# A fused MLP kernel: other load order, packed transpose banks and late tail transposes in its first 10 microseconds

## The chip, the cores and the metric

The kernel runs on one core of one Trainium2 chip. The metric is the device time of one execution in microseconds (us), lower is better. Times before and after are medians of several executions. The profile shows one execution; its "span" runs from the first to the last instruction on the core and is about 1.7 to 2.2 us shorter than the device time. Engines: PE (matmul), PEld (weight load), DVE (VectorE), ACT (ScalarE), POOL (GpSimd), SP (SyncE, which here issues loads). SBUF and PSUM are the memories named in the code: in these kernels operands lie in SBUF tiles, and PE's results in PSUM tiles, from where other engines copy them.

## The reference

```python
B, S, D, F = 1, 2048, 576, 4608          # all bf16
def reference(x, w1, b1, w2, b2):
    h = jnp.einsum("bsd,df->bsf", x, w1) + b1
    r = jnp.where(h > 0, h, 0)
    h = r * r
    return jnp.einsum("bsf,fd->bsd", h, w2) + b2
```

## The kernel before

The 2048 rows are worked in four blocks of 512. Each block's x must stand transposed in SBUF (tile `xT`, 576 = four chunks of 128 columns and a tail of 64). For blocks 1 to 3 the DMA transposes. Block 0 is loaded plainly and transposed on PE, by intent so that the first matmuls can start early (in the first trace plain x loads landed 2.9 to 3.4 us after issue, DMA transposes 4.0 us, medians). The first group of w1 columns (four blocks of 128, tile `w1n`) is multiplied chunk by chunk while chunks arrive, half of the rows at a time; its 64-row tail is done last by four "tail matmuls", which use 64 rows of the array (64*128 in the timeline below), two at a time (in the first trace both of a pair started at 9.85 us, and both of the next within 0.01 us at 10.07 and 10.08). Then come the other 32 column blocks ("w1 rows", tile `w1_h`), done wholly in such 64-row pairs. For those pairs each 64-column piece of x must stand in both halves of the partitions: DVE duplicates them (`dup_windows`).

The parts that the argument touches (cut, `...` marks cuts):

```python
WARM = [512] * 6 + [128]                       # warm-up matmuls on constants
...
load_x(nc.sync, 0);   load_x(nc.scalar, 1)
load_w1n(nc.sync, 0); load_x(nc.scalar, 2)
load_w1n(nc.sync, 1); load_x(nc.sync, 3)
for k in range(2, NK): load_w1n(nc.sync, k)
...
def dup_windows(sb):
    xT = xT_blk[sb]
    keep(nc.vector.tensor_copy(out=xT[0:H, SPC:SPC + 4, :], in_=xT[H:P, E3:E3 + 4, :]))
    keep(nc.vector.tensor_copy(out=xT[H:P, SPC:SPC + 4, :], in_=xT[0:H, O:O + 4, :]))
...
                # first group; x_transpose(j, k): row tile j, column chunk k; k == NK is the tail
                for j in range(2):
                    for k in range(NK): x_transpose(j, k)
                for j in range(2): x_transpose(j, NK)
                x_copies(0)                    # 3 copies on DVE, 2 on ScalarE
                part(0, 0)                     # part(half of the rows, chunk): 4 matmuls
                for k in range(NK + 1): x_transpose(2, k)
                part(0, 1); part(0, 2)
                for k in range(NK + 1): x_transpose(3, k)
                x_copies(1)
                dup_windows(0)
                part(0, 3); part(1, 0)
                make_b1T()                     # bias transposed on PE
                for k in range(1, NK): part(1, k)
                ...                            # pair(i): the tail matmuls, then evacuation
```

(The lines with several calls are joined here to save room.)

Of the kernel before, what the change touches and what calls it, by code (L numbers as in the profile page):

```python
# [11 lines left out]
BF16 = mybir.dt.bfloat16  # L12
FP32 = mybir.dt.float32
# [4 lines left out]
def kernel(  # L18
# [9 lines left out]
    nc = tc.nc  # L28
    keep = tc.keep_in_program_order
    P = 128  # L30
    H = 64
    x2 = x.flatten_outer_dims()
    out2 = out.flatten_outer_dims()
    S, D = x2.shape
    F = w1.shape[1]
    NFT = F // P
    NC = D // H
    NK = NC // 2
    G = 4
    GW = G * P  # L40
# [4 lines left out]
    RT = SB // P  # L45
    DT = P
    DM = D - DT

    const = ctx.enter_context(tc.tile_pool(name="const", bufs=1))
    wpool = ctx.enter_context(tc.tile_pool(name="wpool", bufs=1))  # L50
# [5 lines left out]
    ps_h = ctx.enter_context(tc.tile_pool(name="ps_h", bufs=4, space=PSUM))  # L56
    ps_o = ctx.enter_context(tc.tile_pool(name="ps_o", bufs=4, space=PSUM))

    wps = ps_o.tile([P, 512], FP32, name="wps", tag="po")
    ones = nc.const_aps.tensor(1.0, [P, 512], BF16)  # L60
    WARM = [512] * 6 + [128]
    for i, n in enumerate(WARM):
        keep(nc.tensor.matmul(wps[:, 0:n], lhsT=ones[:, 0:P], rhs=ones[:, 0:n], start=True, stop=True))  # L63

    xs = const.tile([P, RT, D], BF16, name="x_sb")
    w1n = wpool.tile([P, NK, GW], BF16, name="w1n")
    w1n8 = wpool.tile([P, G // 2, P], BF16, name="w1n8")
    w1_h = wpool.tile([P, NC, FH], BF16, name="w1_h")
    w1_v = w1.rearrange("(c p) f -> p c f", p=H)

    def load_x(eng, rt):
        keep(eng.dma_start(out=xs[:, rt, :], in_=x2[rt * P:(rt + 1) * P, :]))

    def load_w1n(eng, k):
        keep(eng.dma_start(out=w1n[:, k, :], in_=w1[k * P:(k + 1) * P, 0:GW]))

    def load_w1n8(eng, h):
        src = w1[NK * P:D, 0:GW].rearrange("p (i h f) -> p i h f", h=2, f=P)
        keep(eng.dma_start(out=w1n8[h * H:(h + 1) * H, :, :], in_=src[:, :, h, :]))

    def load_w1(eng, h, j0, j1):
        keep(eng.dma_start(out=w1_h[h * H:(h + 1) * H, :, j0 * P:j1 * P],
                      in_=w1_v[:, :, GW + h * FH + j0 * P:GW + h * FH + j1 * P]))

    load_x(nc.sync, 0)
    load_x(nc.scalar, 1)
    load_w1n(nc.sync, 0)
    load_x(nc.scalar, 2)
    load_w1n(nc.sync, 1)
    load_x(nc.sync, 3)  # L90
    for k in range(2, NK):
        load_w1n(nc.sync, k)

    ident = const.tile([P, P], BF16, name="ident")
    make_identity(nc, ident[:])
    b1_rows = const.tile([P, P], BF16, name="b1_rows")
    nc.gpsimd.memset(b1_rows[:], 0.0)
    nc.gpsimd.dma_start(out=b1_rows[0:NFT, :], in_=b1.rearrange("(ft p) -> ft p", p=P))
    b2_col = const.tile([P, 1], BF16, name="b2_col")
    nc.gpsimd.dma_start(out=b2_col[:], in_=b2[DM:D].rearrange("(d o) -> d o", o=1))  # L100
    b2T = const.tile([P, 1], FP32, name="b2T")
    nc.gpsimd.tensor_copy(out=b2T[:], in_=b2_col[:])
    warm = const.tile([P, 1], FP32, name="warm")
    keep(nc.scalar.activation(out=warm[:], in_=nc.const_aps.tensor(0.0, [P, 1], FP32), func=ACT.Relu))

    E3, O, SPC, E = 0, 1, 5, 6
    LO_W = [O, O + 1, O + 2, O + 3, E, E + 1, E + 2, E3, SPC]
# [9 lines left out]
# [4 lines that stand above are left out]
# [7 lines left out]

    w2_sb = wpool.tile([P, NFT, D], BF16, name="w2_sb")
    w2_view = w2.rearrange("(ft p) d -> p ft d", p=P)  # L130
    W2CH = 9

    def load_w2(c):
        keep(nc.sync.dma_start(out=w2_sb[:, c * W2CH:(c + 1) * W2CH, :], in_=w2_view[:, c * W2CH:(c + 1) * W2CH, :]))
# [3 lines left out]
    alloc_xT(0)  # L138
    xT0 = xT_blk[0]
    HS = SB // 2  # L140
    tb_po = [ps_o.tile([P, 2, HS], BF16, name="tb", tag="po") for _ in range(2)]
    tb_ph = [ps_h.tile([P, 2, HS], BF16, name="tb", tag="ph") for _ in range(4)]
    half_banks = [tb_ph, None]

    def x_transpose(j, k):
        h, q = divmod(j, 2)
        qc = slice(q * P, (q + 1) * P)
        bank, slot, c0 = (half_banks[h][k], 0, k * P) if k < NK else (half_banks[h][2], 1, D - P)
        keep(nc.tensor.transpose(bank[:, slot, qc], xs[:, j, c0:c0 + P], ident[:]))  # L149

    def x_copies(h):
        hc = slice(h * HS, (h + 1) * HS)
        for k in range(NK):
            src = half_banks[h][k][:, 0, :]
            if k % 2 == 0:
                keep(nc.vector.tensor_copy(out=xT0[:, O + k, hc], in_=src))  # L156
            else:
                keep(nc.scalar.copy(out=xT0[:, O + k, hc], in_=src))
        keep(nc.vector.tensor_copy(out=xT0[:, E3, hc], in_=half_banks[h][2][:, 1, :]))


    b1T = const.tile([P, NFT], FP32, name="b1T")

    def make_b1T():
        b1T_ps = ps_o.tile([P, P], BF16, name="b1T_ps", tag="po")
        keep(nc.tensor.transpose(b1T_ps[:], b1_rows[:], ident[:]))  # L166
        keep(nc.vector.tensor_copy(out=b1T[:], in_=b1T_ps[:, 0:NFT]))

    hTs = {}

# [24 lines left out]
    def a_full(sb, order):  # L195
        xT = xT_blk[sb]
        banks = []
        for g in range(G):
            pool, tag = (ps_o, "po") if g < 2 else (ps_h, "ph")
            banks.append(pool.tile([P, SB], FP32, name="pn", tag=tag))  # L200

        def pair(i, start, stop):
            keep(nc.tensor.matmul(banks[2 * i][:], lhsT=w1n8[0:H, i, :], rhs=xT[0:H, SPC, :],  # L203
                             start=start, stop=stop, skip_group_check=order == "k_outer"))
            keep(nc.tensor.matmul(banks[2 * i + 1][:], lhsT=w1n8[H:P, i, :], rhs=xT[H:P, E3, :],  # L205
                             start=start, stop=stop, skip_group_check=order == "k_outer"))

        def full(g, k, start, stop):
            keep(nc.tensor.matmul(banks[g][:], lhsT=w1n[:, k, g * P:(g + 1) * P], rhs=xT[:, O + k, :],  # L209
                             start=start, stop=stop))  # L210

        if order == "rows_first":
            for i in (1, 0):
                pair(i, True, False)
            for g in (2, 3, 0, 1):
                for k in range(NK):
                    full(g, k, False, k == NK - 1)
                evac_h(sb, banks[g], g)
        else:
            if order == "k_outer":  # L220
                tb_new = [ps_h.tile([P, 2, HS], BF16, name="tb", tag="ph") for _ in range(2)]
                half_banks[1] = tb_new + tb_po

                def part(h, k):
                    hc = slice(h * HS, (h + 1) * HS)
                    for g in range(G):
                        keep(nc.tensor.matmul(banks[g][:, hc], lhsT=w1n[:, k, g * P:(g + 1) * P],  # L227
                                              rhs=xT[:, O + k, hc], start=(h == 0 and k == 0), stop=False,
                                              skip_group_check=True))

                for j in range(2):
                    for k in range(NK):
                        x_transpose(j, k)
                for j in range(2):
                    x_transpose(j, NK)
                x_copies(0)
                part(0, 0)
                for k in range(NK + 1):
                    x_transpose(2, k)
                part(0, 1)  # L240
                part(0, 2)
                for k in range(NK + 1):
                    x_transpose(3, k)
                x_copies(1)
                dup_windows(0)
                part(0, 3)
                part(1, 0)
                make_b1T()
                for k in range(1, NK):
                    part(1, k)  # L250
            else:
                for g in (2, 3, 0, 1):
                    for k in range(NK):
                        full(g, k, k == 0, False)
            for i in (1, 0):
                pair(i, False, True)
                evac_h(sb, banks[2 * i], 2 * i)
                evac_h(sb, banks[2 * i + 1], 2 * i + 1)
# [35 lines left out]
    for (j0, j1) in [(0, 1), (1, 2), (2, 4), (4, 6), (6, 8), (8, 10), (10, 12)]:  # L294
        load_w1(nc.sync, 0, j0, j1)
        load_w1(nc.sync, 1, j0, j1)
        if j0 == 0:
            load_w1n8(nc.sync, 0)
            load_w1n8(nc.sync, 1)
    load_xT(1)  # L300
    for (j0, j1) in [(12, 14), (14, 16)]:
        load_w1(nc.sync, 0, j0, j1)
        load_w1(nc.sync, 1, j0, j1)
    keep(nc.sync.dma_start(out=b2_bc[:], in_=b2.partition_broadcast(P)))
    for c in (0, 2, 1, 3):
        load_w2(c)
    load_xT(2)

# [51 lines left out]
```

## Time and profile before

| | |
|---|---|
| time, first three runs | 291.02 us median (290.59 to 291.36) |
| span of the profiled run | 289.6 us |
| PE busy | 285.5 us, 99% of the span |
| tail matmuls of the first group start | 9.85 us |

The page's first part for the kernel before (busy time, share of the span, instructions), and its chain that ended last:

```profile
PE 285.5 (99%) x2027; PEld 139.9 (48%) x2032; DVE 78.6 (27%) x176; ACT 96.7 (33%) x154; POOL 2.3 (1%) x10
...
PE 98%; DMA 1%; issue 0%; DVE 0%
```

PE is the bound, almost without gaps. Only the start, before the dense stream of pairs, leaves room. This is the timeline of the kernel before from 3.3 to 11.2 us. Columns: start in us, duration in us, engine, source line, operation, output<-input, shapes, count of merged instructions, and in brackets how long the engine sat idle and what released it. PEld, load issues and the stream of w1 rows are left out.

```profile
3.77 1.25 PE L149 MATMUL tb<-ident,x_sb 128*128 128x128 bf16 x10 [0.17 <-DMA x_sb<-in_x_dram]
4.53 0.29 DVE L156 COPY xTw<-tb 128x256 bf16<-128x256 bf16 x1 [4.53 <-PE tb L149]
...
4.87 1.01 PE L227 MATMUL pn<-xTw,w1n 128*128 128x256 bf16 x4
...
7.24 0.44 PE L149 MATMUL tb<-ident,x_sb 128*128 128x128 bf16 x5
...
7.92 0.28 DVE L159 COPY xTw<-tb 128x256 bf16<-128x256 bf16 x1
...
8.31 0.69 DVE L119 COPY xTw<-xTw 64x2048 bf16<-64x2048 bf16 x1
...
8.44 1.47 PE L227 MATMUL pn<-xTw,w1n 128*128 128x256 bf16 x12
9.03 0.69 DVE L120 COPY xTw<-xTw 64x2048 bf16<-64x2048 bf16 x1
...
9.85 0.39 PE L203 MATMUL pn<-xTw,w1n 64*128 64x512 bf16 x1
```

Three things are to be read. Four 128x256 matmuls took 1.01 us at 4.87 us, but twelve took only 1.47 us at 8.44 us: in between, at 6.5 us by the trace's clock record, PE's clock stepped from half to full (from start to start, 128x256 matmuls took 213, then 109 ns, transposes 107, then 56 ns). The last x transposes (7.24 us) are followed by copies and then by two duplications on DVE. DVE's last duplication ended at 9.72 us, and the tail matmul at 9.85 us shows no idle bracket: DVE was just in time.

### The profile page before, as it was taken

What the parts mean: (1) busy time and instruction counts of PE and PEld (TensorE: products, weight loads), DVE (VectorE), ACT (ScalarE), POOL (GpSimd) and SP (SyncE); (2) the same over time, 40 slices, a digit from 0 to 9 for tenths busy, and PEclk for the clock granted to TensorE, in tenths of its full rate; (3) what the DMA queues carried; (4) which work ended last, traced back from release to release, by engine and by line L of the source; (5) the groups of instructions that cost most, each with busy time, mean ns of one, the idle gap of its engine ahead of it and who ended that gap; (6) DMA issues with size and microseconds to landing.
All of it is one profiled execution on the core that took longest, in us unless ns stands there. A gap on an engine that the chain in (4) does not pass through costs nothing.

```text
span 289.6 us, 4693 instructions
## 1 busy us (share of the span) xinstructions
PE 285.5 (99%) x2027; PEld 139.9 (48%) x2032; DVE 78.6 (27%) x176; ACT 96.7 (33%) x154; POOL 2.3 (1%) x10
## 2 busy tenths in 40 slices
PE   8999999999999999999999999999999999999996
PEld 5544444444444555555544444444444455555555
DVE  1644554444500200000015444444440001100001
ACT  2566666666500000000027666666670000000000
POOL 3000000000000000000000000000000000000000
PEclk9999999999999999999999999999999999999999
DMA  7999999400001200000000000000000110000000
GB/s 198 221 245 188 308 389 212 92 0 2 0 14 25 52 16 18 16 16 18 16 16 2 1 2 0 2 0 2 0 2 0 36 38 16 16 16 19 33 16 18
DMA packets 31605, 16.52 MB, mean 57 GB/s; under 512 B 15700, under 2 KB 31584, under 8 KB 31584
## 3 DMA queue, kind: packets, MB, share of 16 engines
q1 hardware_dynamic: 31232, 15.91, 22.3%
q10 hardware_dynamic: 288, 0.30, 0.4%
q8 instruction: 16, 0.26, 0.4%
q14 instruction: 5, 0.04, 0.0%
q0 software_dynamic: 64, 0.01, 0.0%
HBM read 11.36 MB, written 2.36 MB: 47 GB/s over the span
## 4 chain that ended last, share of the span: by engine, by line
PE 98%; DMA 1%; issue 0%; DVE 0%
PE ph L188 42%; PE po L289 38%; PE pt L270 11%; PE pn L209 4%; PE pn L227 1%; DMA x_sb<-in_x_dram 1%; PE tb L149 1%; PE ph L190 1%; PE pn L203 1%; DVE o_sb L291 0%; PE b1T_ps L166 0%; PE pn L205 0%
## 5 line engine op out<-in xcount | busy, mean ns | idle before, releaser
L190 PE MATMUL ph<-xTw,w_h 64*128 64x512 bf16 x576 | 124.6, 376 | 0.0
L188 PE MATMUL ph<-xTw,w_h 64*128 64x512 bf16 x576 | 124.6, 376 | 0.0
L289 PE MATMUL po<-w_sb,hT 128*128 128x448 bf16 (+2 forms) x612 | 109.4, 341 | 0.0
L176 ACT ACTIVATE r<-ph,b1T 128x512 bf16<-128x512 f32 x128 | 81.1, 685 | 41.6 <-PE ph L190 41.6
L188 PEld LDWEIGHTS <-w_h 64*128 64x128 bf16 x576 | 54.1, 94 | 68.3
L289 PEld LDWEIGHTS <-hT 128*128 128x128 bf16 x612 | 58.5, 98 | 51.0
L177 DVE TENSOR_TENSOR hT<-r 128x512 bf16<-128x512 bf16 x144 | 61.2, 426 | 75.9 <-ACT r L176 75.5
L190 PEld LDWEIGHTS <-w_h 64*128 64x128 bf16 x576 | 54.1, 94 | 0.0
L291 DVE TENSOR_TENSOR o_sb<-po,b_bc 128x448 bf16<-128x448 f32 (+2 forms) x17 | 10.2, 597 | 125.8 <-PE po L289 125.8
L270 PE MATMUL pt<-hT,w_sb 128*128 128x512 bf16 x142 | 31.3, 379 | 0.1
L176 ACT ACTIVATE r<-pn,b1T 128x512 bf16<-128x512 f32 x16 | 10.3, 688 | 61.0 <-PE pn L205 59.6
L270 PEld LDWEIGHTS <-w_sb 128*128 128x128 bf16 x144 | 14.1, 98 | 17.0
L273 ACT ACTIVATE oT<-pt,b2T 128x512 bf16<-128x512 f32 x4 | 2.8, 688 | 28.3 <-PE pt L270 28.3
L209 PE MATMUL pn<-xTw,w1n 128*128 128x512 bf16 x45 | 10.4, 379 | 0.4 <-issue 0.3
L209 PEld LDWEIGHTS <-w1n 128*128 128x128 bf16 x48 | 4.5, 98 | 6.0 <-issue 0.8
L227 PE MATMUL pn<-xTw,w1n 128*128 128x256 bf16 x32 | 4.6, 295 | 0.0
L63 PE MATMUL wps<-const-bfloat16-1.0 128*128 128x512 bf16 (+1 forms) x7 | 2.8, 582 | 0.8 <-PEq L344 0.8
L227 PEld LDWEIGHTS <-w1n 128*128 128x128 bf16 x32 | 3.3, 107 | 0.5
L156 DVE COPY xTw<-tb 128x256 bf16<-128x256 bf16 x4 | 1.1, 292 | 6.7 <-PE tb L149 6.7
L119 DVE COPY xTw<-xTw 64x2048 bf16<-64x2048 bf16 x4 | 2.8, 690 | 0.2
L120 DVE COPY xTw<-xTw 64x2048 bf16<-64x2048 bf16 x4 | 2.7, 687 | 0.1
L149 PE MATMUL tb<-ident,x_sb 128*128 128x128 bf16 x20 | 2.4, 288 | 0.2 <-DMA x_sb<-in_x_dram 0.2
(23 smaller groups left out, 15.2 us busy)
## 6 DMA issues: line engine op xcount, KB each, us to landing
w_sb<-in_w_dram SPq DMA_DIRECT2D x4, 1296.0 KB, 12.7
w_h<-in_w_dram SPq DMA_DIRECT2D x14, 288.0 KB, 6.2
out_dram<-o_sb SPq DMA_DIRECT2D x15, 112.0 KB, 1.7
w_h<-in_w_dram SPq DMA_DIRECT2D x4, 144.0 KB, 3.5
w1n<-in_w_dram SPq DMA_DIRECT2D x4, 128.0 KB, 3.9
out_dram<-ot SPq DMA_DIRECT2D x4, 128.0 KB, 2.0
x_sb<-in_x_dram ACTq DMA_DIRECT2D x2, 144.0 KB, 2.9
x_sb<-in_x_dram SPq DMA_DIRECT2D x2, 144.0 KB, 3.4
```

The costliest lines, as they stand in the source:

```text
L63: keep(nc.tensor.matmul(wps[:, 0:n], lhsT=ones[:, 0:P], rhs=ones[:, 0:n], start=True, stop=True))
L149: keep(nc.tensor.transpose(bank[:, slot, qc], xs[:, j, c0:c0 + P], ident[:]))
L176: keep(nc.scalar.activation(out=r[:], in_=bank[:], func=ACT.Relu, bias=b1T[:, ft:ft + 1], scale=1.0))
L177: keep(nc.vector.tensor_tensor(out=hTs[sb][:, ft, :], in0=r[:], in1=r[:], op=ALU.mult))
L188: keep(nc.tensor.matmul(bx[:], lhsT=w1_h[0:H, LO_C[i], jc], rhs=xT[0:H, LO_W[i], :], start=(i == 0), stop=(i == NC - 1)))
L190: keep(nc.tensor.matmul(by[:], lhsT=w1_h[H:P, UP_C[i], jc], rhs=xT[H:P, UP_W[i], :], start=(i == 0), stop=(i == NC - 1)))
L203: keep(nc.tensor.matmul(banks[2 * i][:], lhsT=w1n8[0:H, i, :], rhs=xT[0:H, SPC, :], start=start, stop=stop, skip_group_check=order == "k_o ...
L209: keep(nc.tensor.matmul(banks[g][:], lhsT=w1n[:, k, g * P:(g + 1) * P], rhs=xT[:, O + k, :], start=start, stop=stop))
L227: keep(nc.tensor.matmul(banks[g][:, hc], lhsT=w1n[:, k, g * P:(g + 1) * P], rhs=xT[:, O + k, hc], start=(h == 0 and k == 0), stop=False, s ...
L270: keep(nc.tensor.matmul(pt[:], lhsT=w2_sb[:, ft, DM:D], rhs=hT[:, ft, :], start=(i == 0), stop=(i == NFT - 1)))
L289: keep(nc.tensor.matmul(po[:, 0:d1 - d0], lhsT=hT[:, ft, jj * P:(jj + 1) * P], rhs=w2_sb[:, ft, d0:d1], start=(i == 0), stop=(i == NFT - 1)))
L291: keep(nc.vector.tensor_tensor(out=o_sb[:, d0:d1], in0=po[:, 0:d1 - d0], in1=b2_bc[:, d0:d1], op=ALU.add))
```

## The change

It reorders the start. x tiles and w1 chunks load in turn on two queues; the tail weights load early; two column chunks share one PSUM bank; the 64 tail columns of two x row tiles go through one transpose (after GpSimd has packed them side by side); and those tail transposes, with the bias, come late in the first group. By intent it saves PE work: 16 x transposes and three for tails and bias, instead of 20 and one. The core of the diff (cut, `...` marks cuts):

```diff
-    WARM = [512] * 6 + [128]
+    WARM = [512] * 6 + [256]
...
-    load_w1n(nc.sync, 0)
-    load_x(nc.scalar, 2)
-    load_w1n(nc.sync, 1)
-    load_x(nc.sync, 3)
-    for k in range(2, NK):
-        load_w1n(nc.sync, k)
+    for k in range(2):
+        load_w1n(nc.sync, k, k + 1)
+        load_x(nc.scalar, 2 + k)
+    load_w1n(nc.sync, 2, 3)
+    load_w1n(nc.scalar, 3, 4)
...
+    for h in range(2):
+        load_w1n8(nc.sync, h)
+    xs8 = const.tile([P, RT, H], BF16, name="xs8")
+    for h in range(2):
+        keep(nc.gpsimd.tensor_copy(out=xs8[:, 2 * h:2 * h + 2, :], in_=xs[:, 2 * h:2 * h + 2, NK * P:D]))
...
-    W2CH = 9
+    W2CH = 18
...
+    def x_transpose(j):
         h, q = divmod(j, 2)
+        hc = slice(h * HS, (h + 1) * HS)
+        for bank in range(2):
+            for k in range(2 * bank, 2 * bank + 2):
+                keep(nc.tensor.transpose(tb[h][bank][:, k % 2, q * P:(q + 1) * P], xs[:, j, k * P:(k + 1) * P], ident[:]))
+            for k in range(2 * bank, 2 * bank + 2) if q == 1 else ():
+                copy = nc.scalar.copy if h == 1 and bank == 1 else nc.vector.tensor_copy
+                keep(copy(out=xT0[:, O + k, hc], in_=tb[h][bank][:, k % 2, :]))
...
+    def dup_windows_first():
+        keep(nc.vector.tensor_copy(out=xT0[0:H, E:E + 3, :], in_=xT0[H:P, O:O + 3, :]))
+        keep(nc.vector.tensor_copy(out=xT0[H:P, SPC:SPC + 4, :], in_=xT0[0:H, O:O + 4, :]))
+        keep(nc.vector.tensor_copy(out=xT0[0:H, E3, :], in_=xT0[H:P, O + 3, :]))
+
+    def tails_and_b1T():
+        tl = ps_h.tile([P, 3, P], BF16, name="tl", tag="ph")
+        for h in range(2):
+            keep(nc.tensor.transpose(tl[:, h, :], xs8[:, 2 * h:2 * h + 2, :], ident[:]))
+        keep(nc.tensor.transpose(tl[:, 2, :], b1_rows[:], ident[:]))
+        x8 = xT0.rearrange("p c (h q t) -> p c h q t", h=2, q=2)
+        for q in range(2):
+            keep(nc.vector.tensor_copy(out=x8[H:P, E3, :, q, :], in_=tl[q * H:(q + 1) * H, 0:2, :]))
+        for q in range(2):
+            keep(nc.vector.tensor_copy(out=x8[0:H, SPC, :, q, :], in_=tl[q * H:(q + 1) * H, 0:2, :]))
+        keep(nc.vector.tensor_copy(out=b1T[:], in_=tl[:, 2, 0:NFT]))
...
                 for j in range(2):
+                    x_transpose(j)
+                for k in range(2):
+                    part(0, k)
+                    x_transpose(2 + k)
+                dup_windows_first()
+                for k in range(2, NK):
+                    part(0, k)
                 part(1, 0)
-                make_b1T()
+                tails_and_b1T()
                 for k in range(1, NK):
                     part(1, k)
```

The tail matmuls read all four pieces that the four new "tail copies" write, and those copies stand behind the three duplications in DVE's order.

More of the change, by code (lines that the diff above doesn't have):

```diff
@@ L57 @@
     ps_o = ctx.enter_context(tc.tile_pool(name="ps_o", bufs=4, space=PSUM))
-    wps = ps_o.tile([P, 512], FP32, name="wps", tag="po")
+    wps = ps_h.tile([P, 512], FP32, name="wps", tag="ph")
     ones = nc.const_aps.tensor(1.0, [P, 512], BF16)
-    WARM = [512] * 6 + [128]
+    WARM = [512] * 6 + [256]
     for i, n in enumerate(WARM):
@@ L66 @@
     w1n = wpool.tile([P, NK, GW], BF16, name="w1n")
-    w1n8 = wpool.tile([P, G // 2, P], BF16, name="w1n8")
+    w1n8 = wpool.tile([P, GW], BF16, name="w1n8")
     w1_h = wpool.tile([P, NC, FH], BF16, name="w1_h")
@@ L72, in load_x, with load_w1n @@
         keep(eng.dma_start(out=xs[:, rt, :], in_=x2[rt * P:(rt + 1) * P, :]))
-    def load_w1n(eng, k):
-        keep(eng.dma_start(out=w1n[:, k, :], in_=w1[k * P:(k + 1) * P, 0:GW]))
+    def load_w1n(eng, k0, k1):
+        src = w1[k0 * P:k1 * P, 0:GW].rearrange("(k p) f -> p k f", p=P)
+        keep(eng.dma_start(out=w1n[:, k0:k1, :], in_=src))
     def load_w1n8(eng, h):
-        src = w1[NK * P:D, 0:GW].rearrange("p (i h f) -> p i h f", h=2, f=P)
-        keep(eng.dma_start(out=w1n8[h * H:(h + 1) * H, :, :], in_=src[:, :, h, :]))
+        keep(eng.dma_start(out=w1n8[h * H:(h + 1) * H, :], in_=w1[NK * P:D, 0:GW]))
     def load_w1(eng, h, j0, j1):
@@ L83, in load_w1 @@
                       in_=w1_v[:, :, GW + h * FH + j0 * P:GW + h * FH + j1 * P]))
+    b1_rows = const.tile([P, P], BF16, name="b1_rows")
+    nc.vector.memset(b1_rows[:], 0.0)
     load_x(nc.sync, 0)
     load_x(nc.scalar, 1)
-    load_w1n(nc.sync, 0)
-    load_x(nc.scalar, 2)
-    load_w1n(nc.sync, 1)
-    load_x(nc.sync, 3)
-    for k in range(2, NK):
-        load_w1n(nc.sync, k)
+    for k in range(2):
[3 more added lines that the diff above has]
+    load_w1n(nc.scalar, 3, 4)
     ident = const.tile([P, P], BF16, name="ident")
     make_identity(nc, ident[:])
-    b1_rows = const.tile([P, P], BF16, name="b1_rows")
-    nc.gpsimd.memset(b1_rows[:], 0.0)
-    nc.gpsimd.dma_start(out=b1_rows[0:NFT, :], in_=b1.rearrange("(ft p) -> ft p", p=P))
-    b2_col = const.tile([P, 1], BF16, name="b2_col")
-    nc.gpsimd.dma_start(out=b2_col[:], in_=b2[DM:D].rearrange("(d o) -> d o", o=1))
-    b2T = const.tile([P, 1], FP32, name="b2T")
-    nc.gpsimd.tensor_copy(out=b2T[:], in_=b2_col[:])
     warm = const.tile([P, 1], FP32, name="warm")
     keep(nc.scalar.activation(out=warm[:], in_=nc.const_aps.tensor(0.0, [P, 1], FP32), func=ACT.Relu))
+    keep(nc.scalar.dma_start(out=b1_rows[0:NFT, :], in_=b1.rearrange("(ft p) -> ft p", p=P)))
+    for h in range(2):
[3 more added lines that the diff above has]
+        keep(nc.gpsimd.tensor_copy(out=xs8[:, 2 * h:2 * h + 2, :], in_=xs[:, 2 * h:2 * h + 2, NK * P:D]))
     E3, O, SPC, E = 0, 1, 5, 6
@@ L140 @@
     HS = SB // 2
-    tb_po = [ps_o.tile([P, 2, HS], BF16, name="tb", tag="po") for _ in range(2)]
-    tb_ph = [ps_h.tile([P, 2, HS], BF16, name="tb", tag="ph") for _ in range(4)]
-    half_banks = [tb_ph, None]
-    def x_transpose(j, k):
+    tb = [[ps_h.tile([P, 4, HS], BF16, name="tb", tag="ph") for _ in range(2)] for _ in range(2)]
+    def x_transpose(j):
         h, q = divmod(j, 2)
-        qc = slice(q * P, (q + 1) * P)
-        bank, slot, c0 = (half_banks[h][k], 0, k * P) if k < NK else (half_banks[h][2], 1, D - P)
-        keep(nc.tensor.transpose(bank[:, slot, qc], xs[:, j, c0:c0 + P], ident[:]))
@@ L151, in x_copies @@
-    def x_copies(h):
         hc = slice(h * HS, (h + 1) * HS)
-        for k in range(NK):
-            src = half_banks[h][k][:, 0, :]
-            if k % 2 == 0:
-                keep(nc.vector.tensor_copy(out=xT0[:, O + k, hc], in_=src))
-            else:
-                keep(nc.scalar.copy(out=xT0[:, O + k, hc], in_=src))
-        keep(nc.vector.tensor_copy(out=xT0[:, E3, hc], in_=half_banks[h][2][:, 1, :]))
-    b1T = const.tile([P, NFT], FP32, name="b1T")
-    def make_b1T():
-        b1T_ps = ps_o.tile([P, P], BF16, name="b1T_ps", tag="po")
-        keep(nc.tensor.transpose(b1T_ps[:], b1_rows[:], ident[:]))
-        keep(nc.vector.tensor_copy(out=b1T[:], in_=b1T_ps[:, 0:NFT]))
+        for bank in range(2):
[4 more added lines that the diff above has]
+                keep(copy(out=xT0[:, O + k, hc], in_=tb[h][bank][:, k % 2, :]))
@@ L198, in a_full @@
         for g in range(G):
-            pool, tag = (ps_o, "po") if g < 2 else (ps_h, "ph")
+            pool, tag = (ps_o, "po") if g < 2 or order == "k_outer" else (ps_h, "ph")
             banks.append(pool.tile([P, SB], FP32, name="pn", tag=tag))
         def pair(i, start, stop):
-            keep(nc.tensor.matmul(banks[2 * i][:], lhsT=w1n8[0:H, i, :], rhs=xT[0:H, SPC, :],
+            keep(nc.tensor.matmul(banks[2 * i][:], lhsT=w1n8[0:H, 2 * i * P:(2 * i + 1) * P], rhs=xT[0:H, SPC, :],
                              start=start, stop=stop, skip_group_check=order == "k_outer"))
-            keep(nc.tensor.matmul(banks[2 * i + 1][:], lhsT=w1n8[H:P, i, :], rhs=xT[H:P, E3, :],
+            keep(nc.tensor.matmul(banks[2 * i + 1][:], lhsT=w1n8[H:P, (2 * i + 1) * P:(2 * i + 2) * P], rhs=xT[H:P, E3, :],
                              start=start, stop=stop, skip_group_check=order == "k_outer"))
@@ L220, in a_full @@
             if order == "k_outer":
-                tb_new = [ps_h.tile([P, 2, HS], BF16, name="tb", tag="ph") for _ in range(2)]
-                half_banks[1] = tb_new + tb_po
                 def part(h, k):
@@ L231, in a_full @@
                 for j in range(2):
-                    for k in range(NK):
-                        x_transpose(j, k)
-                for j in range(2):
-                    x_transpose(j, NK)
-                x_copies(0)
-                part(0, 0)
-                for k in range(NK + 1):
-                    x_transpose(2, k)
-                part(0, 1)
-                part(0, 2)
-                for k in range(NK + 1):
-                    x_transpose(3, k)
-                x_copies(1)
-                dup_windows(0)
-                part(0, 3)
+                    x_transpose(j)
[5 more added lines that the diff above has]
+                    part(0, k)
                 part(1, 0)
-                make_b1T()
+                tails_and_b1T()
                 for k in range(1, NK):
@@ L296 @@
         load_w1(nc.sync, 1, j0, j1)
-        if j0 == 0:
-            load_w1n8(nc.sync, 0)
-            load_w1n8(nc.sync, 1)
     load_xT(1)
@@ L303 @@
         load_w1(nc.sync, 1, j0, j1)
+    b2_col = const.tile([P, 1], BF16, name="b2_col")
+    keep(nc.sync.dma_start(out=b2_col[:], in_=b2[DM:D].rearrange("(d o) -> d o", o=1)))
+    b2T = const.tile([P, 1], FP32, name="b2T")
+    keep(nc.gpsimd.tensor_copy(out=b2T[:], in_=b2_col[:]))
     keep(nc.sync.dma_start(out=b2_bc[:], in_=b2.partition_broadcast(P)))
-    for c in (0, 2, 1, 3):
+    for c in range(2):
         load_w2(c)
```

## The prediction

> What bounds it now. The page puts PE at 99% of a 289.6 us span, and the chain that ended last at 98% PE. From 9.85 us, when the four row-tiled tail matmuls of the first group start, the PE stream is dense to the end, and the change leaves its matmuls alone. Only the start can move. By the timeline the first transpose starts when x tile 0 lands (3.73 us), the tail matmuls at 9.85 us, the first w1 rows at 10.29 us; PE idles under 0.3 us in between. The trace's clock record says half clock until 6.5 us, full after; start-to-start distances agree (transpose 107, then 56 ns; 128x256 matmul 213, then 109 ns). So the start is PE work, half of it cold; no large wait can be removed.
>
> What changes.
> 1. PE work: 20 transposes and the bias one become 16 plus three. That saves about 0.2 us cold and 0.1 us warm, and adds 0.11 us. But the first two removed ones filled the wait for the first copy.
> 2. Bank copies: in the trace, the copy of the two-slot bank (5.06 us) started only after the last transpose into that bank (4.71 + 0.31 us), although it reads the other slot. With two k's per bank the first copy waits for the second k: 4.63 instead of 4.53 us, and the first matmul group starts near 4.97, not 4.87.
> 3. Loads: x tile 3 lands earlier (6.07 us now), w1 chunks 2 and 3 about as now (6.5 and 7.05 us), just in time. w1 rows keep about 1 us of margin (landed at 13.2, first used near 14.2 us). w2 in two chunks is off the path (needed at 76 us).
> 4. DVE decides it. Now: two 64x2048 duplications (0.69 us each, 0.72 apart) ended at 9.72 us, just in time for 9.85. After: copies of half 1 end about 7.6 us; duplications of 1536, 2048 and 512 columns (estimated 0.56 + 0.69 + 0.29 us from the measured 0.69) run to about 9.3; then four PSUM tail copies at about 0.21 us spacing (as the measured 128x256 ones) end near 10.1 to 10.2. [...] The tail matmuls need all four, while PE reaches them near 9.8: a new PE wait of 0.2 to 0.4 us.
>
> Sum. Tail matmuls at about 10.1 (9.85 before), everything behind unchanged: +0.2 us. The clock step falls at a varying place ([...] only one step, at 6.5 us, is seen here). With an early step both kernels wait for loads and end about equal; with a late one the new kernel loses up to 0.45 us. Three runs before spread over 0.8 us.
>
> Predicted: 291.2 us, 8 in 10 between 290.5 and 291.9. Faster by over 2%: 0.01; within 2%: 0.98; slower by over 2%: 0.01.
>
> Right if the profile shows: first 128x256 matmul near 4.97 us; x tile 3 landed before 6 us; PE idle 0.2 to 0.4 us before the tail matmuls, released by a DVE tail copy; first w1 rows near 10.5 us; no other PE waits.
>
> Wrong if: [...] a w1 chunk or row lands late; tail copies run much slower or faster than 0.21 us; GpSimd's 64-column copies hold the tail transposes.

Three passages are cut where it is marked, because no trace or run shows what they said: one on PSUM operands in point 4, one on the clock step, and one condition of "Wrong if" about a later clock step. Tail matmuls at 10.1 instead of 9.85 us, about +0.2 us, on the 291.02 us then measured gives 291.2 us. What is said of early and late clock steps was the author's estimate: the one trace then at hand shows one step, at 6.5 us, and the later traces show it between 3.4 and 9.7 us. The durations 0.56 and 0.29 us of the new duplications can't be worked out from 0.69 us alone; the trace after measured 0.56, 0.69 and 0.29 us.

## The result and the profile after

The new kernel took 291.63 us (median of six, 291.34 to 291.80), the one before in the same rounds and the first three runs 290.93 us (median of six, 290.46 to 291.36). The ratio is 1.0025, with a 95% interval of 1.0012 to 1.0038. Ratios here are the mean time of one kernel's fast runs over that of the other's of the same rounds, so they are not quite the ratio of the medians. It is a small loss of about 0.7 us on this chip. All experiment runs were correct, and all runs whose state could be told were fast.

The page of the new kernel, the same two parts:

```profile
PE 285.4 (99%) x2030; PEld 144.3 (50%) x2030; DVE 79.8 (28%) x182; ACT 95.9 (33%) x152; POOL 1.5 (1%) x9
...
PE 96%; DVE 1%; ACTq 1%; ACT 0%; DMA 0%; issue 0%; DVEq 0%
```

PE's busy time did not move, but DVE has entered the chain that ended last. The timeline shows where:

```profile
3.50 1.06 PE L148 MATMUL tb<-ident,x_sb 128*128 128x128 bf16 x8
...
4.73 0.71 PE L227 MATMUL pn<-xTw,w1n 128*128 128x256 bf16 x4 [0.17 <-DMA b_rows<-in_b_dram]
...
6.15 0.39 PE L148 MATMUL tb<-ident,x_sb 128*128 128x128 bf16 x4
...
6.46 0.49 DVE L151 COPY xTw<-tb 128x256 bf16<-128x256 bf16 x2 [1.19 <-PE tb L148]
...
7.06 0.56 DVE L156 COPY xTw<-xTw 64x1536 bf16<-64x1536 bf16 x1
...
7.63 0.69 DVE L157 COPY xTw<-xTw 64x2048 bf16<-64x2048 bf16 x1
...
7.85 1.47 PE L227 MATMUL pn<-xTw,w1n 128*128 128x256 bf16 x12
8.33 0.29 DVE L158 COPY xTw<-xTw 64x512 bf16<-64x512 bf16 x1
8.63 0.59 DVE L167 COPY xTw<-tl 64x256 bf16<-64x256 bf16 x2
9.24 0.59 DVE L169 COPY xTw<-tl 64x256 bf16<-64x256 bf16 x2
...
9.88 0.37 PE L206 MATMUL pn<-xTw,w1n 64*128 64x512 bf16 x1 [0.56 <-DVE xTw L169]
```

The last x transposes come 1.1 us earlier than in the first trace (6.15 against 7.24 us). But DVE then works almost without a pause from 6.46 to 9.83 us, and PE sits idle 0.56 us before the tail matmuls, released by the last tail copy. (The 0.17 us before the first 128x256 matmul is put down to a DMA; the program has that matmul wait for DVE's first copy, which ended 0.05 us before it.)

The two spans are equal (289.6 us), although the kernels differ by 0.7 us on average. The two profiled runs are not alike: the clock stepped at 6.5 us in the old kernel's trace and at 5.1 us in the new one's (the spacing of the 128x256 matmuls falls to 109 ns there). So one trace against one trace doesn't give the difference. What does is this: behind the start of the tail matmuls the rest is constant. Span minus that start was 279.75 us in both traces of the unchanged old kernel and 279.68 us in the two of the new one. In the other traces of the new kernel's variants it was 279.67 to 279.69 us, except for side_parts_undone with 279.90; new_loads_on_before had 279.82. So the span of a timed run tells when its tail matmuls started, to about 0.1 to 0.2 us.

### The profile page after: what moved, and what is told of

Read it like the earlier page. It is cut to its first block, busy times and chain, and to the rows that moved or that the text cites. A ratio compares the mean times of both kernels' runs of the same rounds, so it can differ in the third digit from the quotient of the medians.

```text
span 289.6 us, 4701 instructions
## 1 busy us (share of the span) xinstructions
PE 285.4 (99%) x2030; PEld 144.3 (50%) x2030; DVE 79.8 (28%) x182; ACT 95.9 (33%) x152; POOL 1.5 (1%) x9
## 4 chain that ended last, share of the span: by engine, by line
PE 96%; DVE 1%; ACTq 1%; ACT 0%; DMA 0%; issue 0%; DVEq 0%
PE ph L191 41%; PE po L281 38%; PE pt L262 11%; PE pn L212 4%; PE ph L193 2%; PE pn L206 1%; PE pn L227 0%; ACTq L72 0%; ACT L98 0%; DVE xTw L157 0%; DMA b_rows<-in_b_dram 0%; DVE xTw L169 0%; DVE xTw L167 0%; DVE xTw L156 0%; DVE xTw L151 0%
## 5 line engine op out<-in xcount | busy, mean ns | idle before, releaser
L283 DVE TENSOR_TENSOR o_sb<-po,b_bc 128x448 bf16<-128x448 f32 (+2 forms) x17 | 10.1, 597 | 125.8 <-PE po L281 125.8
L206 PE MATMUL pn<-xTw,w1n 64*128 64x512 bf16 x8 | 2.4, 376 | 0.6 <-DVE xTw L169 0.6
L208 PE MATMUL pn<-xTw,w1n 64*128 64x512 bf16 x8 | 2.4, 379 | 0.0
```

The lines of the kernel that those rows point to most:

```text
L206: keep(nc.tensor.matmul(banks[2 * i][:], lhsT=w1n8[0:H, 2 * i * P:(2 * i + 1) * P], rhs=xT[0:H, SPC, :], start=start, stop=stop, skip_grou ...
L283: keep(nc.vector.tensor_tensor(out=o_sb[:, d0:d1], in0=po[:, 0:d1 - d0], in1=b2_bc[:, d0:d1], op=ALU.add))
```

## The experiments

Every run is on one chip with the kernel before: before_again, tails_first, tails_on_act and extra_tails chip 12; tails_two_tiles, old_loads, new_loads_on_before and side_parts_undone chip 0; the other four chip 2. The record doesn't name the chip of the first rounds. Among the experiments the unchanged new kernel ran on chip 2 only (after_again), so for the others its 1.0025 is a figure from other rounds. Twelve were made. Theories: A, PE waits for DVE's tail copies; B, the loads or the clock cost the time; further ones as they came up.

### before_again: is the first trace typical?

No edit.

> The kernel before, unchanged, for a second trace. Theory A (the new kernel is held at a fixed time by its DVE chain, while the old one gains when the clock step comes early): with a clock step earlier than 6.5 us its tail matmuls start up to 0.9 us before the 9.85 us of the first trace (the spread of its six times, 290.46 to 291.36, is 0.9 us); with a step near 6.5 us at 9.85 again. Theory B (the start is fixed by the loads, not by the clock): 9.8 to 9.9 us whatever the clock.

The clock stepped at 6.06 us and the tail matmuls started at 9.51 us (span 289.3 us, one run, state unknown). Eleven timed runs of the old kernel on that chip had spans of 288.8 to 289.5 us, mean 289.15, so their tail matmuls started at 9.1 to 9.8 us, 9.40 on average (span minus 279.75); by the same reckoning the averages of eleven runs on chips 0 and 2 are 9.50 and 9.65. The new kernel's first six runs had spans of 289.6 to 289.9 us, mean 289.77: 9.9 to 10.2 us, 10.09 on average (minus 279.68). The trace that the prediction was made from, 9.85 us, is late for the old kernel, not its middle. The lines of before_again:

```profile
3.54 1.25 PE L149 MATMUL tb<-ident,x_sb 128*128 128x128 bf16 x10
...
6.89 0.44 PE L149 MATMUL tb<-ident,x_sb 128*128 128x128 bf16 x5
...
9.51 0.39 PE L203 MATMUL pn<-xTw,w1n 64*128 64x512 bf16 x1
```

This fits theory A in direction only: the start came 0.34 us earlier, but not by the clock alone, since x tile 0 also landed 0.24 us earlier (3.49 against 3.73 us) and the first transpose began as much earlier (3.54 against 3.77 us).

### tails_first: the tail copies ahead of the duplications

```diff
@@ -235,7 +235,7 @@
                     x_transpose(2 + k)
+                part(0, 2)
+                tails_and_b1T()
                 dup_windows_first()
-                for k in range(2, NK):
-                    part(0, k)
+                part(0, 3)
                 part(1, 0)
-                tails_and_b1T()
                 for k in range(1, NK):
```

> The new kernel with the tail transposes, the four tail copies and the bias cast ahead of the three duplications instead of behind them. Theory A (PE waits 0.56 us for DVE's tail copies before the tail matmuls): the wait goes, tail matmuls near 9.3 us instead of 9.88, time about 0.6 us under the new kernel, ratio to before 1.0000 to 1.0008. Theory B (loads or the clock cost the 0.7 us): ratio stays near 1.0025.

The ratio was 0.9994 (0.9982 to 1.0006), median 290.61 against 290.94 us, a little under what theory A expected. Its timeline:

```profile
6.18 0.49 DVE L151 COPY xTw<-tb 128x256 bf16<-128x256 bf16 x2 [1.27 <-PE tb L148]
...
7.07 0.59 DVE L167 COPY xTw<-tl 64x256 bf16<-64x256 bf16 x2 [0.40 <-PE tl L164]
7.67 0.59 DVE L169 COPY xTw<-tl 64x256 bf16<-64x256 bf16 x2
8.29 0.20 DVE L170 CAST b1T<-tl 128x36 f32<-128x36 bf16 x1
8.52 0.56 DVE L156 COPY xTw<-xTw 64x1536 bf16<-64x1536 bf16 x1
9.10 0.69 DVE L157 COPY xTw<-xTw 64x2048 bf16<-64x2048 bf16 x1
...
9.14 0.39 PE L206 MATMUL pn<-xTw,w1n 64*128 64x512 bf16 x1
...
9.82 0.29 DVE L158 COPY xTw<-xTw 64x512 bf16<-64x512 bf16 x1
```

The same DVE work now runs past the tail matmuls, and PE starts them without an idle bracket. (The tail transposes moved forward too. But in the new kernel they and the bias were done at 8.01 us, 0.6 us before DVE began the tail copies at 8.63 us, so they weren't what was late.) The duplications are first needed by the later pairs of the w1 rows, which did not wait. Theory A is borne out: only the order was changed, and the wait in the trace and the loss against before went away. The unchanged new kernel was not among these rounds. Part of the step to 0.9994 may be luck of the clock step (3.4 us in this trace).

### tails_on_act: two of the four tail copies on ScalarE

```diff
@@ -168,3 +168,3 @@
         for q in range(2):
-            keep(nc.vector.tensor_copy(out=x8[0:H, SPC, :, q, :], in_=tl[q * H:(q + 1) * H, 0:2, :]))
+            keep(nc.scalar.copy(out=x8[0:H, SPC, :, q, :], in_=tl[q * H:(q + 1) * H, 0:2, :]))
         keep(nc.vector.tensor_copy(out=b1T[:], in_=tl[:, 2, 0:NFT]))
```

> The new kernel with two of its four tail copies on ScalarE, order otherwise unchanged. Theory A: DVE's chain is shorter by two copies of 0.30 us, tail matmuls near 9.3 us, time about 0.6 us under the new kernel (ratio 1.0000 to 1.0008). Theory B: ratio near 1.0025.

This missed what theory A expected (1.0000 to 1.0008): the loss stayed, with a ratio of 1.0039 (1.0026 to 1.0052). The timeline shows why the copies did not move side by side:

```profile
8.34 0.59 DVE L167 COPY xTw<-tl 64x256 bf16<-64x256 bf16 x2
...
9.02 0.74 ACT L169 COPY xTw<-tl 64x256 bf16<-64x256 bf16 x2 [2.09 <-DVE xTw L167]
9.80 0.19 DVE L170 CAST b1T<-tl 128x36 f32<-128x36 bf16 x1 [0.86 <-ACT xTw L169]
9.81 0.37 PE L206 MATMUL pn<-xTw,w1n 64*128 64x512 bf16 x1 [0.78 <-ACT xTw L169]
```

ScalarE waited for DVE's last tail copy, then took 0.74 us for what DVE does in 0.59 us, and PE's wait grew to 0.78 us. Both engines read one PSUM tile, and by the trace ScalarE waited for DVE there (2.09 us of idle, ended by DVE's copies of line 167). Why two reads of one tile came one after the other is not shown.

### tails_two_tiles: the same with a PSUM tile for each engine

```diff
@@ -164,2 +164,5 @@
         keep(nc.tensor.transpose(tl[:, 2, :], b1_rows[:], ident[:]))
+        tl2 = ps_h.tile([P, 2, P], BF16, name="tl2", tag="ph")
+        for h in range(2):
+            keep(nc.tensor.transpose(tl2[:, h, :], xs8[:, 2 * h:2 * h + 2, :], ident[:]))
         x8 = xT0.rearrange("p c (h q t) -> p c h q t", h=2, q=2)
@@ -168,3 +171,3 @@
         for q in range(2):
-            keep(nc.vector.tensor_copy(out=x8[0:H, SPC, :, q, :], in_=tl[q * H:(q + 1) * H, 0:2, :]))
+            keep(nc.scalar.copy(out=x8[0:H, SPC, :, q, :], in_=tl2[q * H:(q + 1) * H, 0:2, :]))
         keep(nc.vector.tensor_copy(out=b1T[:], in_=tl[:, 2, 0:NFT]))
```

> As tails_on_act, but the two ScalarE copies read a PSUM tile of their own, filled by two more transposes (0.11 us of PE). In tails_on_act the first ScalarE copy had a wait for DVE and started 0.09 us after DVE's second tail copy ended, so the copies ran one after another. Theory A with that correction: ScalarE copies now run beside DVE's duplications, tail matmuls near 9.4 us, ratio to before 1.0000 to 1.0012. Rival (the ScalarE copies themselves, or PSUM access from two engines, cost the time): ratio stays near 1.004.

The ratio was 0.9999 (0.9985 to 1.0014). The timeline:

```profile
8.09 0.28 PE L167 MATMUL tl<-ident,xs 128*128 128x128 bf16 x2
...
8.40 0.75 ACT L172 COPY xTw<-tl 64x256 bf16<-64x256 bf16 x2 [0.94 <-PE tl L167]
8.57 0.29 DVE L158 COPY xTw<-xTw 64x512 bf16<-64x512 bf16 x1
8.88 0.59 DVE L170 COPY xTw<-tl 64x256 bf16<-64x256 bf16 x2
...
9.61 0.39 PE L209 MATMUL pn<-xTw,w1n 64*128 64x512 bf16 x1
```

ScalarE now copies while DVE duplicates, DVE's chain is two copies shorter, and PE's wait is gone, for two more transposes on PE. The output tile is shared in both runs, so the wait in tails_on_act came from the shared PSUM tile, not from ScalarE as such (ScalarE's idle time was 2.09 us there, ended by DVE, and 0.94 us here, ended by PE's transposes). In time the gain is less clear: old_loads below, on the same chip and with the 0.56 us wait in its trace, had 1.0007 (0.9993 to 1.0021), a difference of 0.23 us in the means with overlapping intervals.

### extra_tails: more of the suspected cost

```diff
@@ -168,2 +168,4 @@
         for q in range(2):
+            keep(nc.vector.tensor_copy(out=x8[H:P, E3, :, q, :], in_=tl[q * H:(q + 1) * H, 0:2, :]))
+        for q in range(2):
             keep(nc.vector.tensor_copy(out=x8[0:H, SPC, :, q, :], in_=tl[q * H:(q + 1) * H, 0:2, :]))
```

> The new kernel with the first two tail copies done twice: two more DVE copies of 0.30 us each in the suspected chain, same result. Theory A: tail matmuls near 10.5 us, time 0.6 us over the new kernel, ratio to before about 1.0045. Theory B: ratio near 1.0025.

The ratio was 1.0040 (1.0026 to 1.0053). In its trace the wait grew to 1.08 us:

```profile
9.24 0.59 DVE L171 COPY xTw<-tl 64x256 bf16<-64x256 bf16 x2
...
9.88 0.37 PE L208 MATMUL pn<-xTw,w1n 64*128 64x512 bf16 x1 [1.08 <-DVE xTw L171]
```

The start of the tail matmuls followed the last x transposes by 4.39 us (5.49 to 9.88), against 3.73 us in the new kernel (6.15 to 9.88): two extra copies made it 0.66 us longer. That its tail matmuls start at the same 9.88 us as in the new kernel's trace goes with the last x transposes, which came 0.66 us earlier in this trace (5.49 against 6.15 us): the clock stepped at 3.5 us, and w1 chunk 1 landed at 4.87 us instead of 5.65. In the mean of six runs the span was 290.32 us, 0.55 us over the new kernel's 289.77 (in other rounds). The firmest comparison of times is with tails_first, on the same chip: 1.0040 against 0.9994, intervals apart, 1.3 us in the means, where theory A expected about 1.2 (0.6 saved, 0.6 added).

### old_loads, old_loads_again, new_loads_on_before, after_again: the load order

On the new kernel (old_loads; old_loads_again is the same file):

```diff
@@ -88,7 +88,8 @@
     load_x(nc.scalar, 1)
-    for k in range(2):
+    load_w1n(nc.sync, 0, 1)
+    load_x(nc.scalar, 2)
+    load_w1n(nc.sync, 1, 2)
+    load_x(nc.sync, 3)
+    for k in range(2, NK):
         load_w1n(nc.sync, k, k + 1)
-        load_x(nc.scalar, 2 + k)
-    load_w1n(nc.sync, 2, 3)
-    load_w1n(nc.scalar, 3, 4)
 
```

On the kernel before (new_loads_on_before):

```diff
@@ -89,5 +89,5 @@
     load_w1n(nc.sync, 1)
-    load_x(nc.sync, 3)
-    for k in range(2, NK):
-        load_w1n(nc.sync, k)
+    load_x(nc.scalar, 3)
+    load_w1n(nc.sync, 2)
+    load_w1n(nc.scalar, 3)
 
```

> The new kernel with the load order of the one before for x and the w1 chunks. Theory A: x tile 3 lands about 0.2 us later, the transposes of the second half and DVE's chain behind them move by that much: 0.1 to 0.3 us slower than the new kernel, ratio to before 1.003 to 1.0035. Theory B (the new load order costs the 0.7 us): ratio near 1.000.

> The kernel before with the new order of the x and w1 loads alone. Theory A: its tail matmuls follow PE work, x tile 3 was not waited for, so within 0.2 us of before, ratio 0.9995 to 1.0005. Theory B: ratio near 1.0025.

> The new kernel unchanged, on one chip with the three below, for a direct comparison. Spans near 289.8 us on average, that is tail matmuls near 10.1 us (in the traces so far the span is 279.68 us longer than the start of the tail matmuls for every form of the new kernel), ratio to before 1.0018 to 1.0030.

> A repeat of old_loads, which missed its expectation (1.0007 instead of 1.003 to 1.0035). Theory L (the new load order is itself slower: w1 chunk 1 landed at 4.71 us in old_loads and at 4.87 to 5.65 in four traces of the new order, x tile 3 at 5.28 against 5.16 to 5.92, so the second-half transposes and DVE's chain start later): ratio 1.0003 to 1.0013, at least 0.0008 under after_again. Rival (chance, different chips): equal to after_again within 0.0005.

old_loads gave 1.0007 (0.9993 to 1.0021): a miss for theory A, as the new kernel had 1.0025 in other rounds. new_loads_on_before gave 0.9996 (0.9982 to 1.0010). The repeat on one chip settled it: after_again 1.0011 (0.9994 to 1.0027), old_loads_again 1.0008 (0.9992 to 1.0025), mean times 291.46 and 291.40 us. So theory L falls too; the load order has no effect that these runs can see, on either kernel. In five of the six traces that leave the new kernel's DVE chain untouched (new or old loads, warm_128 below among them), PE's wait was the same 0.56 us; the sixth, side_parts_undone below, had its clock step late and no wait. Here are its lines in the timelines of after_again and old_loads_again:

```profile
9.72 0.37 PE L206 MATMUL pn<-xTw,w1n 64*128 64x512 bf16 x1 [0.56 <-DVE xTw L169]
```

```profile
10.24 0.37 PE L207 MATMUL pn<-xTw,w1n 64*128 64x512 bf16 x1 [0.56 <-DVE xTw L170]
```

The same unchanged new kernel thus measured 1.0025 in its first rounds and 1.0011 here. The intervals overlap; the mean difference was 0.26 us here, where the old kernel's eleven runs spread from 288.7 to 290.2 us of span.

### tails_first_old_loads: both together

This is tails_first with the load order of old_loads.

> Both repairs together: tails before duplications, and the load order of before. If the DVE wait and the load order are separate losses: faster than before, ratio 0.9983 to 0.9995. If the load order matters only through DVE's chain: as tails_first alone, 0.9990 to 0.9998.

The ratio was 0.9996 (0.9981 to 1.0012), mean 291.05 us against 291.46 us of after_again on the same chip. That is 0.41 us less, with overlapping intervals. It is as tails_first: the old load order adds nothing that can be seen. Neither version can be told from the kernel before.

### side_parts_undone and warm_128: the rest of the change

```diff
@@ -60,3 +60,3 @@
     ones = nc.const_aps.tensor(1.0, [P, 512], BF16)
-    WARM = [512] * 6 + [256]
+    WARM = [512] * 6 + [128]
     for i, n in enumerate(WARM):
@@ -96,2 +96,5 @@
     make_identity(nc, ident[:])
+    b2_col = const.tile([P, 1], BF16, name="b2_col")
+    nc.gpsimd.dma_start(out=b2_col[:], in_=b2[DM:D].rearrange("(d o) -> d o", o=1))
+    b2T = const.tile([P, 1], FP32, name="b2T")
     warm = const.tile([P, 1], FP32, name="warm")
@@ -105,2 +108,3 @@
 
+    nc.gpsimd.tensor_copy(out=b2T[:], in_=b2_col[:])
     E3, O, SPC, E = 0, 1, 5, 6
@@ -130,3 +134,3 @@
     w2_view = w2.rearrange("(ft p) d -> p ft d", p=P)
-    W2CH = 18
+    W2CH = 9
 
@@ -292,8 +296,4 @@
         load_w1(nc.sync, 1, j0, j1)
-    b2_col = const.tile([P, 1], BF16, name="b2_col")
-    keep(nc.sync.dma_start(out=b2_col[:], in_=b2[DM:D].rearrange("(d o) -> d o", o=1)))
-    b2T = const.tile([P, 1], FP32, name="b2T")
-    keep(nc.gpsimd.tensor_copy(out=b2T[:], in_=b2_col[:]))
     keep(nc.sync.dma_start(out=b2_bc[:], in_=b2.partition_broadcast(P)))
-    for c in range(2):
+    for c in (0, 2, 1, 3):
         load_w2(c)
```

> The new kernel with three side parts put back: w2 in four loads, 128 columns in the last warm-up matmul, the small output bias loaded by GpSimd early. Theory A: none of them is on the path, ratio within 0.0008 of the new kernel's 1.0025. Theory C (one of the side parts costs the time, for instance the warm-up through the clock step): ratio near 1.000.

The ratio was 1.0041 (1.0018 to 1.0064), because two of six runs had spans of 291.5 and 291.9 us; the other four were at 289.8 to 290.5, and alone they give about 1.0029, within what theory A expected. The profiled run is one of the two. Its clock stepped at 9.69 us, so its twelve 128x256 matmuls were slow (1.47 us in the kernels above):

```profile
3.97 1.04 PE L152 MATMUL tb<-ident,x_sb 128*128 128x128 bf16 x8 [0.37 <-DMA x_sb<-in_x_dram]
...
7.69 2.46 PE L231 MATMUL pn<-xTw,w1n 128*128 128x256 bf16 x12
...
11.60 0.37 PE L210 MATMUL pn<-xTw,w1n 64*128 64x512 bf16 x1
```

(The next expectation counts 0.57 us of idle time where the profile has 0.37.) The tail matmul has no idle bracket: with PE at half clock until 9.69 us, PE's own work lasted as long as DVE's tail copies, which ended at 11.54 us.

Putting the side parts back did not win anything, so theory C falls as a cause of the loss. The run showed a late clock step instead, with x tile 0 landing at 3.92 us. The warm-up alone was tried next (the last warm-up matmul back to 128 columns):

```diff
@@ -60,3 +60,3 @@
     ones = nc.const_aps.tensor(1.0, [P, 512], BF16)
-    WARM = [512] * 6 + [256]
+    WARM = [512] * 6 + [128]
     for i, n in enumerate(WARM):
```

> The new kernel with the last warm-up matmul at 128 columns as before. In side_parts_undone two of six runs had spans of 291.5 and 291.9 us, and the profiled one had its clock step at 9.69 us, [...] with PE idle for 0.57 us before the first transpose. Theory W [...]: one or more of the runs over 291.3 us span, the rest as after_again. Rival (the early load of the output bias delayed x tile 0, and that made the gap): no such run.

(Theory W is that the shorter warm-up brings the late step. Two passages are cut; until then all other traces had their step at 3.4 to 6.5 us.)

It gave 1.0011 (0.9994 to 1.0027) with no span over 290.1 us, the same as after_again. Theory W, in the form that the shorter warm-up is enough, falls. That the small GpSimd load delayed x tile 0 (3.92 us there, 3.73 in the first trace), and with it the step, was the author's estimate: no run isolates it.

### All traces by clock step

The table takes the clock step from the trace's clock record, or from the matmul spacing, to about 0.1 us, where the record is missing. "Last transposes" is the start of those of x row tile 3. The last column is taken before rounding to 0.01 us or after, so it can be off by that.

| trace | clock step | last transposes | tail matmuls | last transposes to tail matmuls |
|---|---|---|---|---|
| before | 6.5 | 7.24 | 9.85 | 2.61 |
| before_again | 6.1 | 6.89 | 9.51 | 2.61 |
| new_loads_on_before | 4.7 | 6.52 | 9.13 | 2.61 |
| new kernel | 5.1 | 6.15 | 9.88 | 3.73 |
| after_again | 5.1 | 5.98 | 9.72 | 3.74 |
| warm_128 | 5.2 | 6.02 | 9.76 | 3.74 |
| old_loads | 4.4 | 5.82 | 9.55 | 3.73 |
| old_loads_again | 6.2 | 6.51 | 10.24 | 3.73 |
| side_parts_undone | 9.7 | 7.26 | 11.60 | 4.34 |
| tails_on_act | 4.8 | 5.86 | 9.81 | 3.95 |
| extra_tails | 3.5 | 5.49 | 9.88 | 4.39 |
| tails_two_tiles | 5.9 | 6.39 | 9.61 | 3.22 |
| tails_first | 3.4 | 5.87 | 9.14 | 3.28 |
| tails_first_old_loads | 6.7 | 6.78 | 9.89 | 3.11 |

At equal clock step the new kernel is behind. At 5.1 us the old form would start its tail matmuls near 9.24 us (an estimate, on the line between its traces at 4.7 and 6.1), the new one's three traces say 9.72 to 9.88: 0.5 to 0.6 us. At 6.2 us the estimate for the old form is 9.61, and old_loads_again has 10.24: 0.6 us. (This second estimate leans late, because x tile 0 was late in the trace before, one end of its line.) That is close to PE's wait of 0.56 us.

## Why the prediction was right or wrong

The predicted 291.2 us (290.5 to 291.9) held the measured 291.63 us, and "within 2%" was right. Point by point:

1. **What bounds it.** Right: only the start moved; what follows the tail matmuls kept its length (279.75 and 279.68 us).
2. **PE work, bank copies.** Right in kind. In the trace after, the first copy began at 4.39 us, just behind the end (4.35 us) of the last transpose into its bank, and the first matmul came 1.23 us after the first transpose, against 1.10 us before. The predicted 4.97 us was 4.73 us because the transposes began 0.27 us earlier in that run (x tile 0 landed at 3.33 us instead of 3.73).
3. **Loads.** x tile 3 landed at 5.92 us, before 6 us as said, but the old order had it at 5.24 us in before_again. The order made no difference that the runs could see, on either kernel. The small waits of PE on w1 chunks in the traces after (0.2 us on chunk 1 in the first) were not among the signs listed.
4. **DVE decides it.** Right, and the experiments show it: PE waited for a DVE tail copy; moving those copies forward, or half of them to ScalarE with a PSUM tile of its own, removed the wait in the traces, and neither version can be told from the kernel before; doing two of them twice raised wait and time. On one chip, tails_first and extra_tails differ clear of noise. The size was off. The step "four PSUM tail copies at about 0.21 us spacing (as the measured 128x256 ones)" failed: they came at 0.30 us. The profile shows both pairs, 0.49 us for two 128x256 copies and 0.59 us for two tail copies of the same length, so two ordinary copies overlap and two tail copies don't. From the end of half 1's copies to the end of the last tail copy DVE took 2.9 us (6.95 to 9.83), where the prediction had 2.5 to 2.6 (7.6 to 10.1 or 10.2). The wait was 0.56 us instead of 0.2 to 0.4. From start to start it was 0.30 us at a duration of 0.28 to 0.30 us for the tail copies, and 0.20 to 0.21 us at 0.28 to 0.29 us for the ordinary ones: 0.09 us more for each. What kept the tail copies apart is not shown: their inputs alternate between partitions 0 and 64, those of the ordinary copies don't, and they have another shape (64x256 against 128x256); no run changed either alone.
5. **The sum.** The step "Tail matmuls at about 10.1 (9.85 before)" failed in its second half. The new kernel's first six runs give 10.09 us on average, by span. That is partly luck, since the too short tail copies were made up for by a clock step earlier than assumed (in the one profiled of these runs; of the others the step isn't known). The old kernel gives 9.40, 9.50 and 9.65 us on the three chips with eleven runs. The profiled run, with the clock step at 6.5 us, was the slowest of the four times then known (291.46 us), and its 9.85 us was set beside a median of 291.02 us. The term was 0.25 us in the prediction; by the times of the first rounds it was 0.7 us, by the spans on chip 2 0.3 (9.65 against 9.97), by traces at equal clock step 0.5 to 0.6 us.
6. **The clock.** That the step falls at a varying place was right: thirteen of the fourteen traces have it between 3.4 and 6.7 us, side_parts_undone at 9.69 us. "With an early step both kernels ... end about equal" was wrong: with steps near 5 us the new kernel was behind by an estimated 0.5 to 0.6 us (no trace of the old form has a step before 4.7 us). From the last transposes to the tail matmuls the new kernel took 3.73 us with steps at 4.4, 5.1 and 6.2 us, the old form 2.61 with steps at 4.7, 6.1 and 6.5, all of them before those transposes. "With a late one the new kernel loses up to 0.45 us" has no support either: in the one trace with a late step, side_parts_undone, PE shows no wait for DVE before the tail matmuls. So these traces show the wait with an early step and not with a late one, the reverse of what was predicted; no trace of the old form with a late step exists to compare.

What stays open is the exact size: 1.0025 and 1.0011 were measured for the same kernel in two sets of rounds, and the second interval includes 1. On chips 0 and 2, taking the wait away was worth 0.2 to 0.4 us in the means, less than the 0.56 us of the traces and within the noise.

## What to carry to other kernels

When work moves off PE, follow the engine that must prepare PE's next operands: here PE's stream was hardly shorter, but four small copies now stood last in DVE's queue, in front of the matmuls that needed them, behind duplications that nobody needed yet. Order a preparing engine's queue by when its results are read, and give each reading engine its own PSUM tile before splitting copies over engines (here PE's wait was 0.78 us with one shared tile and none with two). And when the effect is under a microsecond, look at where the one profiled run lies among the timed ones before using its times as a baseline.
